# Preparing a block's tokens three blocks ahead, and their remainder behind the second layer's sums

## The chip, the cores and the metric

The kernel runs on one core of a Trainium2 chip. The core has a matrix engine (PE), a vector engine (DVE), an activation engine (ACT), a general engine (POOL), and an engine that issues most DMAs (SP). Each takes its own row of instructions in order; semaphores hold them together. The metric is the device time of one execution in microseconds (us); the median of several is given.

## The reference

Attention with a query averaged over pairs of its rows, then a mixture of eight experts with one expert for each token. `x` is the attention's output as 4608 tokens of 512 values; a token goes through the expert with the highest gate, and the result is scaled by the gate:

```python
q_pool = q.reshape(B, H, S // factor, factor, D).mean(axis=3)
attn = softmax(scale * np.matmul(q_pool, k.transpose(0, 1, 3, 2)))   # in short; written out in the reference
x = (attn @ v).transpose(0, 2, 1, 3).reshape(B * S, H * D)
logits = x @ w_gate + modality_bias[modality_id]
e_idx = np.argmax(logits, axis=1)
for e in range(E):
    mask = e_idx == e
    h = np.maximum(x[mask] @ w1[e], 0.0)          # 512 -> 1024
    out[mask] = gate_w[mask, None] * (h @ w2[e])  # 1024 -> 512
```

## The kernel before

The first 700 us or so are attention. While the last pairs run, the tokens are routed: they are sorted by expert, and two lists of row numbers are made, `giA` for the first eight blocks of 256 tokens and `giB` for the rest. What is left of this routing, and the counting for the later list, is a generator named `side`; `beside()` runs one step of it (a few DVE operations of lines 535 to 547, sometimes a small product of line 580).

The expert stage is `run_blocks` (from line 1828). Blocks 0 to 3 are *plain*: `gemm1` four times, `gemm2` four times, PE in fp16 with every operand split into a high half and a remainder (hi x hi, hi x lo, lo x hi). Blocks 4 to 17 are *seven-product* blocks: 2 x 2 block matrices are multiplied with seven products instead of eight, after sums and differences of the operands have been formed. Block 18 has few tokens and other experts; `general` handles leftovers, of which these inputs have none.

One round of the loop over j (line 1886) is `together(j, j + 1)` and then `tail(j + 1)`. `together` takes the first-layer products 11, s2 and s3 of block j + 1, and the second layer of block j in the order 11, 22, 12, s3, s1, s2, s4 (`second`); `tail` takes the other first-layer products of j + 1: 12, s1, 22 and s4. Each first-layer product is 24 matmuls (line 1605), each second-layer product 12 (line 1705). The order on PE, ACT, DVE and POOL is that in which the code issues; the steps of the generators are placed between the products by the loop. The steps of `together` in the loop are numbered s = 0 to 5; the block's own sums and casts stand between them.

What the other engines do in one round:

- POOL: four subtractions or additions of the hidden values of block j (line 1647, in `tail`), the token differences of a later block (line 1535), sometimes one or two additions of weights (line 1432), two gathers (line 1347, 128 rows each), the sum o of the second layer (line 1739), and two scatters of the finished block's halves (line 1591), with a drain behind the second. A scatter to the output starts when the one before it has landed.
- ACT: the casts to fp16 (line 1613), the copy p of the first product (line 1673), the ReLUs (lines 1623 and 1632), scaled copies of the second layer's products (p, o and x, line 1716), weight halves (line 1425), and for a later block the scaled tokens `xr` (line 1532) and their high half `xs` (line 1539).
- DVE: remainders of the casts (line 1617), sums of the first layer (h22, h12, h21 in line 1622; u2, u3 in lines 1693 and 1694), five sums of the second layer (line 1717), weight remainders (line 1426), and for a later block the token remainder (line 1540).
- SP: weight loads into five buffers, and the two transposes of `xs` into the tile `xpart` (line 1544).

The tokens of a block go through `load_x` (the gathers into `xg`, one buffer of each half) and `turn_s` (from line 1523): step 1 copies the gates and scales the tokens on ACT into `xr`; step 2 forms four differences on POOL; step 3 makes the high half on ACT and the remainder on DVE; step 4 issues the transposes. `xr` and `xs` have one buffer, `xpart` two. In round j the kernel before takes these four steps for block j + 2 at s = 0, 1, 3 and 5 (`T_TURN`) and gathers block j + 3 at s = 3; the gather of block 8, the first that uses the second list, stands behind the tail of the round before, after all of `side`.

Of the kernel before, what the change touches and what calls it, by code (L numbers as in the profile page):

```python
# [105 lines left out]
NSA = 4  # L106
NSB = 5
NA = 2 * NSA
# [4 lines left out]
WR = 5  # L113
JOINED = 2
PREP = ((1,) * 8, ((0, 1, 1, 0, 0, 0),) * 6 + ((0,) * 6, (1,) * 6, (1,) * 6) + ((1, 1, 1, 0, 0, 1),) * 4)
T_TURN = (0, 1, 3, 5)
SIDE = 1
PH = 3
PO = 2
GX = 3  # L120
# [1253 lines left out]
def experts(tc, ctx, rt, ident, pre, x2pool, hip, w1, w2, out, side, first):  # L1374
# [16 lines left out]
    def beside():  # L1391
        for _ in range(SIDE):
            next(side, None)
# [131 lines left out]
    def turn_s(j):  # L1525

        b = B[j]
        gates(j)
        r = xq.tile([P, 8, TB], F32, name="xr")
        for h in (0, 1):  # L1530
            x, sc = scaled_x(j, h)
            nc.scalar.activation(r[:, 2 - 2 * h:4 - 2 * h].rearrange("p k n -> p (k n)"), x, AF.Copy, scale=sc)  # L1532
        yield
        for o, x, y in ((4, 0, 2), (6, 1, 0), (5, 1, 4), (7, 3, 5)):
            nc.gpsimd.tensor_tensor(r[:, o], r[:, x], r[:, y], op=ALU.subtract)  # L1535
        yield
        xs = xq.tile([P, 2, 7 * TB], F16, name="xs")
        flat = r[:, 1:8].rearrange("p k n -> p (k n)")
        nc.scalar.copy(xs[:, 0], flat)
        nc.vector.tensor_tensor(xs[:, 1], flat, xs[:, 0], op=ALU.subtract)  # L1540
        yield
        x = b["xo"] = xq.tile([P, 2, 7, 2, P], F16, name="xpart", bufs=2)
        for w in range(2):
            nc.sync.dma_start_transpose(out=x[:, w].rearrange("p k c n -> p (k c) n"), in_=xs[:, w])
        yield
# [113 lines left out]
        put_hi(j, n, t)  # L1659
        put_lo(j, n, t)  # L1660

    def together(i, j):

        def mine(n):
            if i is not None:
                sums(i, n)

        if j is not None:
            b = B[j]
            pa = b["pa"] = bank()  # L1670
            product1(pa, "11", "11", j, True)
            p1 = temp("p1")
            nc.scalar.copy(p1, pa)
            beside()
            mine("s3")
            pb = b["pb"] = bank()
            product1(pb, "s2", "t2", j, True)
            beside()
            pc = b["pc"] = bank()
            product1(pc, "s3", "t3", j, True)  # L1680
            beside()
            mine("s1")
        else:
            mine("s3")
            mine("s1")
        g = second(i) if i is not None else iter(())
        next(g, None)
        mine("s2")
        next(g, None)
        mine("s4")  # L1690
        if j is not None:
            u2, u3 = b["u2"], b["u3"] = temp("u2"), temp("u3")
            nc.vector.tensor_tensor(u2, pb, p1, op=ALU.add)
            nc.vector.tensor_tensor(u3, pc, u2, op=ALU.add)
        yield
        yield from g
# [127 lines left out]
    def step(g, n=1):  # L1824
        for _ in range(n):
            next(g, None)

    def run_blocks():

        plain = range(NSA)  # L1830
        for j in plain:
            for q in range(4):
                B.setdefault(j, {})["w", q] = first["w", q]
        raws = [load(0, w2, q) for q in range(4)]
        load_x(1)
        turn = {1: turn_x(1)}
        prep = chain(combined(1, w1, sets[0]["w1"], (4, 5, 6, 7, 8, 13, 14)), combined(1, w2, sets[0]["w2"], (15, 16, 17, 18, 19, 20, 0)))
        for j in plain:
            for s in range(8):
                if s < 4:  # L1840
                    if j == 0:
                        for k in plain:
                            B[k]["w", 4 + s] = None
                        w = split(raws[s], 9 + s)
                        for k in plain:
                            B[k]["w", 4 + s] = w
                    gemm1(j, s)
                else:
                    gemm2(j, s % 4)
                if j == 0 and s in (1, 2):  # L1850
                    step(turn[1])
                if j:
                    step(prep, PREP[0][s])
                if j and s == T_ST:
                    scatter(j - 1, 1)
                    nc.gpsimd.drain(fusable=False)
                if s == GX:
                    load_x(j + 2)
                    turn[j + 2] = (turn_x if j + 2 < NSA else turn_s)(j + 2)
                if s in T_AHEAD:  # L1860
                    step(turn[j + 2])
                if j + 1 >= NSA and s < 2:
                    step(turn[j + 1])
            if j + 1 < NSA:
                drain(turn[j + 1])
            scaled(j, 0)
            scaled(j, 1)
            scatter(j, 0)
        drain(prep)
        j = NSA  # L1870
        drain(turn[j])
        last = NST - 1
        change = NSA + NSA + NSB
        for k in range(NSA, NST):
            B.setdefault(k, {}).update(sets[k >= change])
        drain(together(None, j))
        scatter(j - 1, 1)
        drain(turn[j + 1])
        load_x(j + 2)
        for _ in tail(j):  # L1880
            beside()
        nc.gpsimd.drain(fusable=False)
        prep = chain(combined(0, w1, sets[1]["w1"], (1, 2, 3, 9, 10, 11, 12)), combined(0, w2, sets[1]["w2"], (7, 8, 6, 13, 5, 4, 14)), few_weights())
        few_x_ = few_x()
        few1, few2 = few_first(NST), few_second(NST)
        for j in range(NSA, NST):
            if j == last:
                drain(few1)
            if j + 2 <= last and j + 2 not in turn:
                turn[j + 2] = turn_s(j + 2)  # L1890
            for s, _ in enumerate(together(j, j + 1 if j < last else None)):
                beside()
                if j + 2 <= last and s in T_TURN:
                    step(turn[j + 2])
                if s == 3 and j + 3 <= last and j + 3 != NA:
                    load_x(j + 3)
                if j == last - 1:
                    step(few_x_)
                step(prep, PREP[1][j - NSA][s] if j < last else 0)
                if s == 4:  # L1900
                    scatter(j, 1)
            if j < last:
                for s, _ in enumerate(tail(j + 1)):
                    beside()
                    beside()
                    if s == 0:
                        scatter(j, 0)
                        nc.gpsimd.drain(fusable=False)
                if j + 3 == NA:
                    drain(side)  # L1910
                    load_x(j + 3)
        scatter(last, 0)
        nc.gpsimd.drain(fusable=False)
        drain(few2)
# [141 lines left out]
```

## Time and profile before

| what | value |
|---|---|
| median of 3 runs | 1205.84 us (1201.77 to 1206.2) |
| the profiled execution's own time | 1206.51 us |
| its span in the trace | 1204.8 us |
| PE busy over the span | 1076.6 us, 89% |
| DVE, ACT, POOL busy | 969.9, 872.8, 623.1 us (81%, 72%, 52%) |
| mean clock granted to PE | 0.961 of full speed |

The shares are averages over two different stages. Up to about 775 us PE is busy all the time; from there on it is busy 60 to 80% of each stretch, and all the other engines are idle for a part of each block. In such a stage the shares say little: one looks for what ended each wait of PE, and follows that back. A row of the trace reads: start in us, duration in us, engine, line, operation, output<-inputs; in brackets the idle time of the engine just before, and what ended it.

### The profile page before, as it was taken

The numbers are of one execution on the slowest core, as the hardware profiler recorded it, in microseconds if no ns is written. First come the engines' busy times: TensorE is split into PE (matmuls) and PEld (weight loads), VectorE is DVE, ScalarE is ACT, GpSimd is POOL, SyncE is SP. The second block draws the span as 40 slices with busy tenths as digits, with TensorE's granted clock in tenths as the row PEclk, the third lists the DMA queues.
The fourth block names the chain that finished last, engine by engine and source line by source line (L and its number), as shares of the span: only waits on it lengthen the run. The fifth ranks groups of instructions, "written<-read, shape, count | busy, mean of one in ns | idle before, by whom it ended". The sixth has DMA issues, their size and how long they took to land. (4 is left out here: it accounts for less than half of the span.)

```text
span 1204.8 us, 39654 instructions
## 1 busy us (share of the span) xinstructions
PE 1076.6 (89%) x16809; PEld 865.5 (72%) x16809; DVE 969.9 (81%) x1778; ACT 872.8 (72%) x1506; POOL 623.1 (52%) x610
## 2 busy tenths in 40 slices
PE   7999999999999999999999999968867778567875
PEld 3777777777777777677777788867756667567774
DVE  7999999999999999999999974895645656466674
ACT  5899999999999999999999964433434544345542
POOL 7755445454544545445453215664556655665533
PEclk9999999999999999999999999998988999789898
DMA  7787887898888789788876744464243224654321
GB/s 224 184 185 199 191 214 185 193 191 178 201 192 210 178 200 185 174 205 188 195 164 140 200 144 125 129 141 82 70 102 66 67 66 102 102 118 102 84 69 37
DMA packets 181868, 180.19 MB, mean 150 GB/s; under 512 B 113999, under 2 KB 144735, under 8 KB 181680
## 3 DMA queue, kind: packets, MB, share of 16 engines
q1 hardware_dynamic: 171414, 149.22, 52.0%
q0 software_dynamic: 10256, 28.33, 10.8%
q8 instruction: 133, 2.18, 0.8%
q14 instruction: 55, 0.45, 0.1%
q10 hardware_dynamic: 10, 0.00, 0.0%
HBM read 100.30 MB, written 18.98 MB: 99 GB/s over the span
## 5 line engine op out<-in xcount | busy, mean ns | idle before, releaser
L1023 ACT ACTIVATE Pe<-psc 128x432 int32<-128x432 f32 x768 | 376.8, 528 | 37.6 <-PE psc L1022 22.9
L1081 PE MATMUL xp<-VH,Pe 128*128 128x65 f16 x2880 | 345.1, 194 | 0.0
L1082 PE MATMUL xp<-vl,Pe 128*128 128x64 f16 x2880 | 343.6, 192 | 0.0
L1083 PE MATMUL xp<-VS,Pl 128*128 128x65 f16 x2880 | 343.1, 193 | 0.3 <-DVE Pl L1006 0.3
L1081 PEld LDWEIGHTS <-Pe 128*128 128x128 f16 x2880 | 266.5, 97 | 92.8 <-issue 49.6
L946 DVE TENSOR_REDUCE mp<-pm 128x2 f32<-128x1024 f32 (+3 forms) x319 | 296.6, 937 | 20.2 <-PE pm L964 16.4
L1021 PE MATMUL psc<-B 128*128 128x432 f16 (+2 forms) x1152 | 302.2, 286 | 0.9 <-ACT Pe L1023 0.8
L1022 PE MATMUL psc<-B 128*128 128x432 f16 (+2 forms) x1152 | 299.6, 285 | 2.7 <-DMA B<-mr 2.7
L1082 PEld LDWEIGHTS <-Pe 128*128 128x128 f16 x2880 | 265.9, 98 | 42.7
L1083 PEld LDWEIGHTS <-Pl 128*128 128x128 f16 x2880 | 266.2, 97 | 0.5 <-DVE Pl L1006 0.5
L1004 ACT ACTIVATE Pl<-Pe 128x1152 f16<-128x1152 uint16 x186 | 216.5, 1164 | 5.9
L867 POOL TENSOR_SCALAR VH<-rawv,sc 128x512 f16<-128x512 f32 (+1 forms) x60 | 104.0, 1734 | 42.6 <-DVE Pl L1006 39.8
L1022 PEld LDWEIGHTS <-B 128*128 128x128 f16 x1152 | 112.5, 98 | 10.8 <-issue 2.8
L1021 PEld LDWEIGHTS <-B 128*128 128x128 f16 x1152 | 111.1, 97 | 7.8 <-issue 2.4
L728 POOL TENSOR_TENSOR rawq<-rawq 128x576 f32<-128x576 f32 x31 | 43.7, 1408 | 119.2 <-DVE Pl L1006 113.7
L775 POOL TENSOR_TENSOR lo<-rawk,hi 128x576 f16<-128x576 f32 (+1 forms) x68 | 81.6, 1221 | 43.1 <-DVE Pl L1006 34.2
L1006 DVE TENSOR_SCALAR Pl<-Pe 128x576 f16<-128x576 uint16 (+1 forms) x198 | 93.2, 472 | 5.7 <-ACT Pe L1023 5.4
L946 DVE TENSOR_REDUCE mp<-xp 128x1 f32<-128x512 f32 x116 | 78.9, 680 | 0.0
L964 PE MATMUL pm<-hi,qh 64*128 64x512 f16 x348 | 70.0, 383 | 1.1 <-DVE mp L946 1.1
L1535 POOL TENSOR_TENSOR xr<-xr 128x256 f32<-128x256 f32 x56 | 52.1, 951 | 32.9 <-ACT xr L1532 31.8
L1623 ACT ACTIVATE h<-h 128x512 f32<-128x512 f32 x42 | 26.4, 629 | 57.0 <-DVE h L1622 56.8
L1647 POOL TENSOR_TENSOR h<-h,h 128x512 f32<-128x512 f32 x42 | 62.3, 1483 | 3.3
(533 smaller groups left out, 2577.4 us busy)
## 6 DMA issues: line engine op xcount, KB each, us to landing
B<-hi SPq DMA_DIRECT2D x128, 144.0 KB
rawv<-in_att_dram SPq DMA_DIRECT2D x32, 576.0 KB
rawq<-in_att_dram SPq DMA_DIRECT2D x31, 576.0 KB
rawk<-in_att_dram SPq DMA_DIRECT2D x31, 576.0 KB
raw<-in_w_dram SPq DMA_DIRECT2D x28, 512.0 KB
B<-qh SPq DMA_DIRECT2D x128, 72.0 KB
B<-lo SPq DMA_DIRECT2D x64, 144.0 KB
xs<-x SPq DMA_DIRECT2D x15, 576.0 KB
```

The costliest lines, as they stand in the source:

```text
L775: done = (nc.gpsimd if p < 2 or i in LO_POOL else nc.vector).tensor_tensor(o[:, r], t[:, r], h[:, r], op=ALU.subtract)
L867: done = nc.gpsimd.tensor_scalar(vh, v, s["sc"], None, op0=ALU.mult)
L946: most = lambda o, x: nc.vector.tensor_reduce(o, x, op=ALU.max, axis=AX.X)
L964: nc.tensor.matmul(banks[to], queries(j, what), hi[half[j], t * 512:(t + 1) * 512], start=True, stop=True)
L1004: nc.scalar.activation(low, rest, AF.Copy, scale=LOW)
L1006: fast[0] = (nc.vector if eng == 'D' else nc.gpsimd).tensor_single_scalar(low, rest, LOW, op=ALU.mult)
L1021: nc.tensor.matmul(o, b1[:, ks], b1[:, qs], start=True, stop=False, skip_group_check=True)
L1022: nc.tensor.matmul(o, b2[:, ks], b2[:, qs], start=False, stop=True, skip_group_check=True)
L1023: nc.scalar.activation(Pe[:, D + x0:D + x1], pt, AF.Exp, scale=1.0 / 16)
L1081: nc.tensor.matmul(out, Ph[:, qs], vh[:, c, j, 0:D + 1], start=c == 0 and g == 0, stop=False, skip_group_check=True)
L1082: nc.tensor.matmul(out[:, 0:D], Ph[:, qs], vl[:, c, j], start=False, stop=False, skip_group_check=True)
L1083: nc.tensor.matmul(out, Pl[:, qs], vs[:, c, j, 0:D + 1], start=False, stop=c == NKC - 1, skip_group_check=True)
```

## The change

`turn_s` yields once more: ACT's high half is one step, and DVE's remainder together with the transposes the next. In round j these steps are now taken for block j + 3. The first, gates and scaling, is handed to `together` as `scaling` and stands right behind the copy p of product 11, ahead of the casts of the round; the differences come at s = 0, the high half at s = 3, the remainder and the transposes at s = 5, behind the second layer's sums. Block j + 4 is gathered at s = 3. For block 8 what is left of `side` is run in front of that gather, in round 4. So that the first rounds find their tokens ready, blocks 4 and 5 are prepared in the plain blocks and block 6 in the round that fills the pipeline, and each step of the plain blocks runs one more step of `side`. In the last rounds there is less to prepare: round 14 gathers nothing, rounds 15 and 16 prepare nothing of this kind.

Because one line was added near the top and two further down, the lines after the change read one to two higher: 1539 is 1540, 1540 is 1542, 1622 is 1623, 1717 is 1719.

```diff
@@ -113,7 +113,8 @@
 WR = 5
 JOINED = 2
 PREP = ((1,) * 8, ((0, 1, 1, 0, 0, 0),) * 6 + ((0,) * 6, (1,) * 6, (1,) * 6) + ((1, 1, 1, 0, 0, 1),) * 4)
-T_TURN = (0, 1, 3, 5)
+T_TURN = (0, 3, 5)
+T_GX = 3
 SIDE = 1
 PH = 3
 PO = 2
@@ -1537,8 +1538,8 @@
         xs = xq.tile([P, 2, 7 * TB], F16, name="xs")
         flat = r[:, 1:8].rearrange("p k n -> p (k n)")
         nc.scalar.copy(xs[:, 0], flat)
+        yield
         nc.vector.tensor_tensor(xs[:, 1], flat, xs[:, 0], op=ALU.subtract)
-        yield
         x = b["xo"] = xq.tile([P, 2, 7, 2, P], F16, name="xpart", bufs=2)
         for w in range(2):
             nc.sync.dma_start_transpose(out=x[:, w].rearrange("p k c n -> p (k c) n"), in_=xs[:, w])
@@ -1659,7 +1660,7 @@
         put_hi(j, n, t)
         put_lo(j, n, t)
 
-    def together(i, j):
+    def together(i, j, scaling=iter(())):
 
         def mine(n):
             if i is not None:
@@ -1672,6 +1673,7 @@
             p1 = temp("p1")
             nc.scalar.copy(p1, pa)
             beside()
+            step(scaling)
             mine("s3")
             pb = b["pb"] = bank()
             product1(pb, "s2", "t2", j, True)
@@ -1836,17 +1838,17 @@
         turn = {1: turn_x(1)}
         prep = chain(combined(1, w1, sets[0]["w1"], (4, 5, 6, 7, 8, 13, 14)), combined(1, w2, sets[0]["w2"], (15, 16, 17, 18, 19, 20, 0)))
         for j in plain:
+            k = j + 2
             for s in range(8):
                 if s < 4:
                     if j == 0:
-                        for k in plain:
-                            B[k]["w", 4 + s] = None
                         w = split(raws[s], 9 + s)
-                        for k in plain:
-                            B[k]["w", 4 + s] = w
+                        for m in plain:
+                            B[m]["w", 4 + s] = w
                     gemm1(j, s)
                 else:
                     gemm2(j, s % 4)
+                beside()
                 if j == 0 and s in (1, 2):
                     step(turn[1])
                 if j:
@@ -1854,13 +1856,21 @@
                 if j and s == T_ST:
                     scatter(j - 1, 1)
                     nc.gpsimd.drain(fusable=False)
-                if s == GX:
-                    load_x(j + 2)
-                    turn[j + 2] = (turn_x if j + 2 < NSA else turn_s)(j + 2)
-                if s in T_AHEAD:
-                    step(turn[j + 2])
-                if j + 1 >= NSA and s < 2:
-                    step(turn[j + 1])
+                if k <= NSA and s == GX:
+                    load_x(k)
+                    turn[k] = (turn_x if k < NSA else turn_s)(k)
+                if s in T_AHEAD and k <= NSA:
+                    step(turn[k])
+                if j == NSA - 1:
+                    if s < 3:
+                        step(turn[NSA])
+                    if s == 0:
+                        load_x(NSA + 1)
+                        turn[NSA + 1] = turn_s(NSA + 1)
+                    if s > 3:
+                        step(turn[NSA + 1])
+                    if s == 6:
+                        load_x(NSA + 2)
             if j + 1 < NSA:
                 drain(turn[j + 1])
             scaled(j, 0)
@@ -1869,16 +1879,23 @@
         drain(prep)
         j = NSA
         drain(turn[j])
+        drain(turn[j + 1])
         last = NST - 1
         change = NSA + NSA + NSB
         for k in range(NSA, NST):
             B.setdefault(k, {}).update(sets[k >= change])
+            if k > NSA + 1:
+                turn[k] = turn_s(k)
         drain(together(None, j))
+        step(turn[j + 2])
+        load_x(j + 3)
+        step(turn[j + 2])
         scatter(j - 1, 1)
-        drain(turn[j + 1])
-        load_x(j + 2)
-        for _ in tail(j):
+        for s, _ in enumerate(tail(j)):
             beside()
+            if s == 1:
+                step(turn[j + 2])
+        drain(turn[j + 2])
         nc.gpsimd.drain(fusable=False)
         prep = chain(combined(0, w1, sets[1]["w1"], (1, 2, 3, 9, 10, 11, 12)), combined(0, w2, sets[1]["w2"], (7, 8, 6, 13, 5, 4, 14)), few_weights())
         few_x_ = few_x()
@@ -1886,14 +1903,15 @@
         for j in range(NSA, NST):
             if j == last:
                 drain(few1)
-            if j + 2 <= last and j + 2 not in turn:
-                turn[j + 2] = turn_s(j + 2)
-            for s, _ in enumerate(together(j, j + 1 if j < last else None)):
+            x = turn.get(j + 3, iter(()))
+            for s, _ in enumerate(together(j, j + 1 if j < last else None, x)):
                 beside()
-                if j + 2 <= last and s in T_TURN:
-                    step(turn[j + 2])
-                if s == 3 and j + 3 <= last and j + 3 != NA:
-                    load_x(j + 3)
+                if s in T_TURN:
+                    step(x)
+                if s == T_GX and j + 4 <= last:
+                    if j + 4 == NA:
+                        drain(side)
+                    load_x(j + 4)
                 if j == last - 1:
                     step(few_x_)
                 step(prep, PREP[1][j - NSA][s] if j < last else 0)
@@ -1906,9 +1924,6 @@
                     if s == 0:
                         scatter(j, 0)
                         nc.gpsimd.drain(fusable=False)
-                if j + 3 == NA:
-                    drain(side)
-                    load_x(j + 3)
         scatter(last, 0)
         nc.gpsimd.drain(fusable=False)
         drain(few2)
```

On DVE, the round of block 13 before (it runs from 1080.70 us on; w15 and w16 are weight halves, xs the token remainder, u and o the second layer's five sums, the last row h22):

```order
L1694 TENSOR_TENSOR u_22468<-ph,u_22467 128x512
L1498 COPY gate<-xg_22162 128x1
L1498 COPY gate<-xg_22164 128x1
L1426 SCALAR_TENSOR_TENSOR w15l<-raw,w15h 128x1024
L1540 TENSOR_TENSOR xs<-xr,xs 128x1792
L1717 SCALAR_TENSOR_TENSOR u_22557<-po_22428,gate,p_22444 128x256
L1717 SCALAR_TENSOR_TENSOR u_22558<-po_22429,gate,u_22557 128x256
L1717 SCALAR_TENSOR_TENSOR o_22427<-po_22429,gate,u_22558 128x256
L1717 SCALAR_TENSOR_TENSOR u_22556<-po_22428,gate,p_22443 128x256
L1717 SCALAR_TENSOR_TENSOR o_22426<-po_22430,gate,u_22556 128x256
L1426 SCALAR_TENSOR_TENSOR w16l<-raw,w16h 128x1024
L1622 TENSOR_TENSOR h_22641<-ph,u_22468 128x512
```

and after the change:

```order
L1696 TENSOR_TENSOR u_22494<-ph,u_22493 128x512
L1427 SCALAR_TENSOR_TENSOR w15l<-raw,w15h 128x1024
L1719 SCALAR_TENSOR_TENSOR u_22576<-po_22454,gate,p_22470 128x256
L1719 SCALAR_TENSOR_TENSOR u_22577<-po_22455,gate,u_22576 128x256
L1719 SCALAR_TENSOR_TENSOR o_22453<-po_22455,gate,u_22577 128x256
L1719 SCALAR_TENSOR_TENSOR u_22575<-po_22454,gate,p_22469 128x256
L1719 SCALAR_TENSOR_TENSOR o_22452<-po_22456,gate,u_22575 128x256
L1542 TENSOR_TENSOR xs<-xr,xs 128x1792
L1427 SCALAR_TENSOR_TENSOR w16l<-raw,w16h 128x1024
L1623 TENSOR_TENSOR h_22661<-ph,u_22494 128x512
```

The remainder (xs) has moved from the front of the five sums to behind them, still ahead of the weight half and of h22, and the two gate copies have left this place.

On ACT, the front of the same round before (p is the copy of product 11, hs3h to hs4h the casts of the hidden sums, xr the scaled tokens):

```order
L1673 COPY p_22366<-ph 128x512
L1613 CAST hs3h<-hs_22331 128x512
L1613 CAST hs1h<-h_22328 128x512
L1716 ACTIVATE p_22443<-po_22428,gate 128x256
L1716 ACTIVATE p_22444<-po_22428,gate 128x256
L1613 CAST hs2h<-h_22237 128x512
L1613 CAST hs4h<-h_22297 128x512
L1532 ACTIVATE xr<-xg_22162 128x512
L1532 ACTIVATE xr<-xg_22164 128x512
```

and after the change:

```order
L1674 COPY p_22386<-ph 128x512
L1533 ACTIVATE xr<-xg_22181 128x512
L1533 ACTIVATE xr<-xg_22183 128x512
L1614 CAST hs3h<-hs_22351 128x512
L1614 CAST hs1h<-h_22348 128x512
L1718 ACTIVATE p_22469<-po_22454,gate 128x256
L1718 ACTIVATE p_22470<-po_22454,gate 128x256
L1614 CAST hs2h<-h_22257 128x512
L1614 CAST hs4h<-h_22317 128x512
```

The two scalings stand now right behind p, ahead of all four casts, and they are those of a block one further ahead.

## Rows read from the trace of the kernel before

**Rows 1.** Two stretches: busy us of PE, PEld, DVE, ACT, POOL; clock, DMA, GB/s.

```profile
750.00:775.00 25.00, 25.00 (x231) 22.41 (x230) 20.89 (x52) 10.42 (x14) 15.36 (x11) 1.00 0.45 138
...
1025.00:1050.00 25.00, 12.26 (x152) 11.96 (x150) 10.92 (x14) 8.30 (x12) 13.14 (x11) 0.66 0.74 122
```

**Rows 2.** Waits of PE from 770 us: line waited for, total us, times, longest.

```profile
PE ph L1605 <- DVE h L1622: 47.0, 10, 9.2
PE ph L1605 <- DMA xpart<-xs: 21.9, 10, 4.1
PE po L1705 <- ACT x L1716: 13.0, 5, 4.9
PE po L1705 <- ACT p L1716: 10.5, 8, 1.9
```

**Rows 3.** PE: starts of two first-layer products.

```profile
794.56 1.50 PE L1605 MATMUL ph<-xpart,xfirst 128*128 128x128 f16 x24
795.90 0.28 PE L1605 MATMUL ph<-xpart,x 128*128 128x128 f16 x2
```

**Rows 4.** PE: starts of two second-layer products in the round of block 13.

```profile
1084.74 0.38 PE L1705 MATMUL po<-x,h12h 128*128 128x256 f16 x2 [1.44 <-ACT p L1716]
...
1086.04 0.38 PE L1705 MATMUL po<-x,hs3h 128*128 128x256 f16 x2
```

**Rows 5.** POOL in other rounds: first subtractions, differences, addition, gather, scatters.

```profile
809.43 1.26 POOL L1647 TENSOR_TENSOR hs<-h,h 128x512 f32<-128x512 f32 x1 [0.33 <-ACT h L1623]
...
823.60 2.90 POOL L1535 TENSOR_TENSOR xr<-xr 128x256 f32<-128x256 f32 x4 [8.37 <-ACT xr L1532]
826.46 2.35 POOL L1432 TENSOR_TENSOR raw<-raw 128x1024 f32<-128x1024 f32 x1
828.95 2.58 POOL L1347 DMA_INDIRECT xg<-xs,giA  x1
...
852.33 4.75 POOL L1535 TENSOR_TENSOR xr<-xr 128x256 f32<-128x256 f32 x4 [1.97 <-ACT xr L1532]
...
1035.57 1.01 POOL L1591 DMA_INDIRECT out_dram<-o,siB  x1 [0.16 <-POOL raw L1432]
1045.55 0.99 POOL L1591 DMA_INDIRECT out_dram<-o,siB  x1 [8.97 <-DMA out_dram<-o,siB]
...
1150.50 0.99 POOL L1591 DMA_INDIRECT out_dram<-o,siB  x1 [0.43 <-DVE u L1717]
1154.13 1.02 POOL L1591 DMA_INDIRECT out_dram<-o,siB  x1 [2.64 <-DMA out_dram<-o,siB]
...
1179.63 1.26 POOL L1647 TENSOR_TENSOR hs<-h,h 128x512 f32<-128x512 f32 x1 [2.00 <-ACT few L1764]
```

**Rows 6.** POOL in the round of block 13, in order of time.

```profile
1080.70 1.26 POOL L1647 TENSOR_TENSOR hs<-h,h 128x512 f32<-128x512 f32 x1 [2.05 <-issue]
1082.03 4.61 POOL L1647 TENSOR_TENSOR h<-h,h 128x512 f32<-128x512 f32 x3
1088.61 3.88 POOL L1535 TENSOR_TENSOR xr<-xr 128x256 f32<-128x256 f32 x4 [1.97 <-ACT xr L1532]
1092.64 0.98 POOL L1347 DMA_INDIRECT xg<-xs,giB  x1
...
1097.33 0.72 POOL L1739 TENSOR_TENSOR o<-x,u 128x256 f32<-128x256 f32 x1 [2.43 <-DVE u L1717]
1098.51 1.00 POOL L1591 DMA_INDIRECT out_dram<-o,siB  x1 [0.46 <-DVE u L1717]
1103.98 0.99 POOL L1591 DMA_INDIRECT out_dram<-o,siB  x1 [4.47 <-DVE h L1622]
1107.03 1.26 POOL L1647 TENSOR_TENSOR hs<-h,h 128x512 f32<-128x512 f32 x1 [2.05 <-issue]
```

**Rows 7.** ACT's copy of the high half in that round.

```profile
1092.52 1.69 ACT L1539 CAST xs<-xr 128x1792 f16<-128x1792 f32 x1 [2.32 <-POOL xr L1535]
```

**Rows 8.** DVE's remainder in that round.

```profile
1094.24 2.02 DVE L1540 TENSOR_TENSOR xs<-xr,xs 128x1792 f16<-128x1792 f32 x1 [3.13 <-ACT xs L1539]
```

## The prediction

> **What bounds the kernel now.** I read the waits of PE from 770 us on first, then the busy time by stretch, then one block instruction by instruction on POOL, ACT, DVE and PE. Before 775 us PE is busy in every microsecond [rows 1], so nothing that other engines do there can shorten the time; the change can win only behind it, in the fourteen seven-product blocks. There PE waits, and the waits have names [rows 2]: ten for a sum h22 on DVE (47.0 us), ten for the transposed tokens of the next block (21.9 us), then ACT's scaled copies x and p (13.0 and 10.5 us). PE has fourteen products in a block: a first-layer product takes 795.90 - 794.56 = 1.34 us, a second-layer one 1086.04 - 1084.74 = 1.30 us [rows 3, 4], together 7 x 1.34 + 7 x 1.30 = 18.5 us. A block takes more: POOL's first subtraction of line 1647 starts at 809.43 us in the first of these blocks and at 1179.63 us in the last [rows 5, 6], thirteen periods in 370.2 us, 28.5 us on average.
>
> The waits on PE are ends of a ring that runs through POOL. In the block that starts at 1080.70 us [rows 6] POOL does its four subtractions (to 1086.64), idles 1.97 us for ACT's scaled tokens, makes four differences of tokens (3.88 us), issues two gathers, idles 2.43 us for DVE's sum u, adds (0.72 us), issues the first scatter at 1098.51, and can issue the second only at 1103.98, when the first has landed. 0.99 us of issue and 2.05 us of drain later the next block begins, at 1107.03. ACT's copy xs waits 2.32 us for those differences [rows 7]; DVE's remainder, 2.02 us after an idle of 3.13 us [rows 8], stands in front of the second layer's five sums, which is why POOL waits for u, and the same five sums stand in front of h22, for which PE waits.
>
> **The change, part by part.** *Scaling ahead of hs3h.* ACT's two scaled copies (the first ends the 1.97 us of idle on POOL) move ahead of four casts. They then lie in the time in which ACT waits for POOL's first subtraction anyway; POOL finds the tokens ready and the 1.97 us goes. *Remainder behind the sums.* DVE does the five sums first, so POOL's 2.43 us for u goes as well: u needs PE's second-layer product s2, the fifth of the stage, whose group ends about 9.3 us after POOL's first subtraction (12 starts 1084.74 - 1080.70 = 4.04 us after it, then four products of 1.30 us), plus two sums, some 10.5 us; POOL itself comes free at 11.95 us (5.94 + 3.4 + 2.6, below). Where there is nothing to gather, u decides. *Transposes a block ahead.* They are issued when PE has left the old tile, a whole block before use; the 21.9 us cannot stay as such. SP's weight loads behind them move by the length of two transposes, and their buffers are used only in the block after. *Gathers.* The same two per block, at the same step, one block further ahead; the one at the change from the first to the second index list, which stood at the end of a block, is now issued in the step of the others. *Side work.* A third call per step in the plain blocks pulls the rest of the routing into a stretch where DVE is busy 20.89 of 25 us and PE 25.00 [rows 1]. Cost: nothing if DVE's 4 us of room in that stretch and the larger room before it take it; at worst the same DVE work stalls PE for a few products, up to 4 us; below zero too, since PE has this work taken off the later blocks. I take 0.
>
> So what is left of a block is POOL's own row of work. Its fixed part: 5.94 (four subtractions) + 0.72 (add) + 0.46 (idle in front of the scatter) + 0.99 + 2.05 = 10.16 us [rows 6]. The four differences cost 2.90 us alone and 4.75 us beside DVE's long operations [rows 5]; they now follow straight on the subtractions, beside two of DVE's casts, so I take 3.4. That these two engines get in each other's way is a rule of the Trainium skill too (GPSIMD Engine Reference, Specifications: the SBUF interfaces are shared with VectorE, with contention where DVE reads two SBUF inputs), and it speaks against the new place, since the casts' remainders read two. By that rule alone each of eleven blocks would pay 4.75, and the time would be 15 us longer than I forecast; the row of 2.90 us shows that the differences also find free time.
>
> Two gathers run from 1092.64 to 1097.33 - 2.43 = 1094.90, 2.6 us with the gaps around them [rows 6]; one of them alone took 2.58 us beside the remainder on DVE, and a weight addition takes 2.35 us [rows 5]. The largest unknown is L, from the first scatter's issue to the second's: 5.47 us in the block shown [rows 6], 3.63 us where no gather ran, 9.98 us in the block with the most weight loads [rows 5]. Today the transposes of the same block run beside that landing; they leave it, but the gathers come nearer. I keep it at about what each kind has today.
> - Four blocks with a gather and no weight addition: 10.16 + 3.4 + 2.6 + L 5.5 = 21.7 us each, 86.7 us.
> - Four with one addition (2.35) and gathers between those two cases (3.3): L 6.2, 25.4 us each, 101.6 us.
> - Two with two additions: 10.16 + 3.4 + 4.7 + 3.5 + L 8.8 = 30.5 us each, 61 us.
> - Two late ones without a gather: u decides, 10.5 + 0.72 + 0.46 + 3.65 + 3.04 = 18.4 us, hardly over PE's 18.5: 19 us each, 38 us.
> - The one before last has no token work today either: 22.5 us stays (from 1154.13 + 1.02 and the 2 us of drain to 1179.63 [rows 5]).
>
> Together 309.8 us against 370.2: 60.4 us less. PE then waits 3 to 7 us in most blocks, in one place (ACT's p, before the product 12). After long waits the granted clock is lower, 0.66 of the full 2.4 GHz on average in the worst stretch [rows 1], which is much of it at the lower level of 1.2 GHz, where a product takes longer; POOL's row covers most of that, and I give back 4 us. Nothing is booked for the attention stage or for the end. The profiled execution took 1206.51 us, of which 1204.8 us is span; its distance to the median 1205.84 us is 0.7 us and I leave it. 1206.5 - 60.4 + 4 = **1150 us**.
>
> **Rivals.** *A: the landing follows the gathers.* In the block shown the second scatter starts 9.1 us after the last gather's issue ends; without a gather it starts 3.63 us after the first scatter. If the scatter's data queue behind the gathers' data, what counts is the gather's end, and the idle for u was free. Then a block is 5.94 + 3.4 + 2.6 + 9 + 3.04 = 24.0 us, with an addition 27.0 us, the two heavy ones 31: 15 us more than forecast, 1165 us. For it: L is long just where gathers stand close. Against it: the transposes that shared that time leave.
> *B: h22 stays late.* The remainder is still ahead of h22 on DVE. Differences at 4.75 us put its end at 5.94 + 4.75 + 1.69 + 2.02 = 14.4 us, against 13.2 us when PE has the first product for h22; with ACT's copy behind x as well, PE would keep about half of the 47.0 us. Only the transposes' 21.9 us and a little more go: 1180 us.
> *C: PE bounds.* If L drops to 3.7 us with the transposes gone, the ten lighter blocks come near PE's 18.5 us: 10 x 18.8 + 61 + 22.5 = 271.5 us, 1108 us.
> *D: slower.* One copy buffer holds the tokens: ACT's copy for the next block must wait until both transposes of the last have landed, and these now stand in SP's row behind PE's tail. ACT takes its work in order, so the split of weights and the ReLU behind that copy wait with it, then h22, the tail and POOL. Differences end 9.3 us into a block, so a landing before that costs nothing. If it comes only 20 us into the block, behind a weight load that waits for its buffer, a block takes some 20 + 1.7 + 2.0 + 8 = 32 us (8 us: from the remainder's end at 1096.26 to 1107.03, less the five sums [rows 6, 8]), in eleven blocks 11 x (32 - 28.5) = 38 us more than now: 1245 us. It turns slower than now from about 17 us. Against it: the old tile is free before the block begins.
> *E: no change.* If POOL's waits just move into L in every block, the period stays: 1201 to 1206 us.
>
> **How the numbers follow.** Forecast 0.47, A 0.20, B 0.11, C 0.10, E 0.07, D 0.05. The likeliest is 1150 us. The range reaches from halfway to C over A to B with its bounds: 1118 to 1185 us; outside are the lower half of C, D and E. Half a percent, 6 us, is about what a measurement of this kernel can tell from no change; faster by more than that has 0.88, within it 0.07, slower 0.05.
>
> **What would show it.** PE's wait for xpart gone from the list; its wait for h22 under 15 us; its wait for ACT's p grown to some 40 us; POOL's idle in front of the differences gone and that for u under 10 us; block periods of 21 to 25 us, with the two heavy blocks near 30. A is right if the second scatter still starts about 9 us after the gathers; B if h22 leads the list; D if ACT idles in front of its copy for a DMA. The forecast is wrong above all if L is not what it was.

## The result, and the profile after

The changed kernel takes 1173.5 us (median of 4 runs, 1170.12 to 1175.51) against 1204.41 us before: a ratio of 0.9742, with a 95% interval of 0.9711 to 0.9774, or 31 us less. The forecast was 1150 us; so the direction and the range held, and the time is 23.5 us above it. The profiled execution took 1172.89 us with a span of 1171.2 us.

PE's waits in the changed kernel from 770 us on, to be held against [rows 2] (line waited for, total, times, longest; a line of before reads one or two higher here):

```profile
PE po L1707 <- ACT p L1718: 33.1, 10, 6.9
PE ph L1606 <- DVE h L1623: 16.1, 7, 8.4
PE po L1707 <- ACT x L1718: 12.8, 4, 5.1
PE ph L1606 <- ACT p L1674: 3.5, 1, 3.5
PE ph L1606 <- DMA xpart<-xs: 2.4, 1, 2.4
```

The wait for the transposes is nearly gone (21.9 us to 2.4 us, one wait), h22 has fallen from 47.0 to 16.1 us, and ACT's p has taken the first place: it comes late because the casts in front of it wait for POOL's first subtraction. So PE's waits have moved to where POOL's row sets the round. POOL in the round of block 13, the same round as [rows 6]:

```profile
1053.54 1.29 POOL L1648 TENSOR_TENSOR hs<-h,h 128x512 f32<-128x512 f32 x1 [2.46 <-ACT h12h L1614]
1054.91 4.62 POOL L1648 TENSOR_TENSOR h<-h,h 128x512 f32<-128x512 f32 x3
1059.50 4.83 POOL L1536 TENSOR_TENSOR xr<-xr 128x256 f32<-128x256 f32 x4
1064.48 0.99 POOL L1348 DMA_INDIRECT xg<-xs,giB  x1 [0.15 <-issue]
1065.77 0.96 POOL L1348 DMA_INDIRECT xg<-xs,giB  x1 [0.30 <-DVE u L1719]
1066.75 0.73 POOL L1741 TENSOR_TENSOR o<-x,u 128x256 f32<-128x256 f32 x1
1067.77 2.50 POOL L1592 DMA_INDIRECT out_dram<-o,siB  x1 [0.28 <-POOL o L1741]
1073.29 1.01 POOL L1592 DMA_INDIRECT out_dram<-o,siB  x1 [3.02 <-DVE h11l L1618]
1078.35 1.26 POOL L1648 TENSOR_TENSOR hs<-h,h 128x512 f32<-128x512 f32 x1 [4.06 <-issue]
```

The two idle times that the change was to remove are removed: nothing lies ahead of the differences (before 1.97 us), nothing ahead of the sum o (before 2.43 us). The first scatter is issued 14.23 us into the round, before 17.81 us. But the round is 24.81 us long, before 26.33 us: of 4.4 us of idle time removed, 1.5 us are left. The rest is lost in two places in these rows. The differences take 4.83 us (before 3.88), and behind the second scatter POOL stands for 4.06 us where it stood for 2.05. The issue of the first scatter is longer as well, 2.50 us (before 1.00), but the second scatter follows the first by 5.52 us, before by 5.47, so that the longer issue is no loss against before in this round; it stands where a gain was to be had, as a later run shows.

The fourteen first subtractions now start at 815.78 to 1142.97 us, thirteen periods in 327.2 us (before 370.2, forecast 309.8). The first of them comes 6.35 us later than before, and from the last to the end of the span it takes 28.2 us, before 25.2.

### The profile page after: what moved, and what is told of

Read it like the earlier page. It is cut to its first block, busy times and chain, and to the rows that moved or that the text cites. A ratio compares the mean times of both kernels' runs of the same rounds, so it can differ in the third digit from the quotient of the medians.

```text
span 1171.2 us, 39664 instructions
## 1 busy us (share of the span) xinstructions
PE 1071.8 (92%) x16809; PEld 857.0 (73%) x16809; DVE 967.6 (83%) x1778; ACT 872.9 (75%) x1506; POOL 639.9 (55%) x610
## 5 line engine op out<-in xcount | busy, mean ns | idle before, releaser
L1536 POOL TENSOR_TENSOR xr<-xr 128x256 f32<-128x256 f32 x56 | 58.1, 1056 | 6.6 <-DVE w20l L1427 2.6
L1618 DVE TENSOR_TENSOR hs3l<-hs,hs3h 128x512 f16<-128x512 f32 x14 | 16.0, 1144 | 50.8 <-ACT hs3h L1614 50.8
```

## The experiments

Each run was measured together with the kernel before, and its ratio is to that kernel, with the 95% interval in brackets. "By the ratios" means: the difference of two ratios times 1204.41 us; it is uncertain by some 5 us.

The theory (T) for the largest of the losses: the drain that POOL does behind the second scatter waits until that scatter has landed, and the transposes, which the change moved to this very moment, lengthen that landing. The rival (S): POOL is held up by DVE on a shared way to memory, and the transposes are bystanders. What spoke for T is the round of block 4 of the changed kernel, on POOL and then on SP:

```profile
834.54 1.02 POOL L1592 DMA_INDIRECT out_dram<-o,siA  x1 [0.28 <-POOL o L1741]
838.16 1.39 POOL L1592 DMA_INDIRECT out_dram<-o,siA  x1 [2.60 <-DVE h22l L1618]
844.02 1.26 POOL L1648 TENSOR_TENSOR hs<-h,h 128x512 f32<-128x512 f32 x1 [4.46 <-issue]
```

```profile
835.98 3.79 SPq L1545 DMA_TRANSPOSE xpart<-xs  x2
```

The second scatter is issued at 838.16 us, while SP is issuing the two transposes (835.98 to 839.77 us); the next subtraction starts 5.86 us later. Of that one scatter the trace gives the time from issue to landing (smallest, median, largest; one instruction):

```profile
DMA to landing us min/median/max: 5.6/5.6/5.6
```

and of its counterpart in the kernel before:

```profile
DMA to landing us min/median/max: 2.7/2.7/2.7
```

In the kernel before the next subtraction started 3.0 to 3.5 us after the second scatter in thirteen rounds, always 0.2 to 0.4 us after it had landed (2.7 to 3.2 us); after the change it starts 3.05 to 5.89 us after it, and in the six rounds whose landing is recorded again 0.2 to 0.4 us behind it. That reads as a landing, and not as a fixed drain of 2 us; the runs that follow try it.

**Transposes held back.** The transposes are a step of their own, issued behind the tail, and wait for POOL's first subtraction of the next round; a block still has a whole round for them.

```diff
             nc.vector.tensor_tensor(xs[:, 1], flat, xs[:, 0], op=ALU.subtract)
+            yield
...
...
+            t = nc.sync.dma_start_transpose(out=x[:, w].rearrange("p k c n -> p (k c) n"), in_=xs[:, w])
+            if "behind" in b:
+                tc.add_manual_dep(t.ins, b["behind"].ins.name, mybir.DependencyInfo(mybir.DependencyClass.Sync, mybir.DependencyReason.DATA))
...
-        sub(b["hs3"], h21, h11)
+        b["first"] = sub(b["hs3"], h21, h11)
...
+                if j + 3 <= last:
+                    B[j + 3]["behind"] = B[j + 1]["first"]
+                step(x)
```

> The changed kernel, with the two transposes of a block held back on SP until POOL's first subtraction of the next round has run, that is until the second scatter and the drain behind it are over; nothing else is moved. Theory T: the drain behind the second scatter waits until that scatter has landed, and the transposes, which now start at the same moment, lengthen that landing from 2.7 to up to 5.6 us; then the time from the second scatter's issue to the next subtraction goes back to about 3.05 us in every round and the kernel takes about 12 us less, 1161 us. Rival S: POOL is held up by VectorE on the shared way to memory, the transposes are bystanders: 1173 us, and the 4 to 6 us behind the second scatter stay.

Measured: 1157.39 us, ratio 0.9624 (0.9581 to 0.9668): 14 us less than the change by the ratios. The round of block 4, on POOL and SP:

```profile
835.00 1.01 POOL L1595 DMA_INDIRECT out_dram<-o,siA  x1 [0.48 <-DVE u L1722]
839.41 1.05 POOL L1595 DMA_INDIRECT out_dram<-o,siA  x1 [3.40 <-DVE h L1626]
842.51 1.27 POOL L1651 TENSOR_TENSOR hs<-h,h 128x512 f32<-128x512 f32 x1 [2.06 <-ACT xr L1533]
```

```profile
843.81 3.68 SPq L1546 DMA_TRANSPOSE xpart<-xs  x2
```

The transposes now start behind the subtraction, and the subtraction follows the second scatter by 3.10 us, as before the change. Over the thirteen rounds the time behind the second scatter falls from 54.9 to 43.4 us. In two rounds it stays above the 3.05 us that were expected (4.01 us in block 6 and 4.78 us in block 14). T holds, S does not.

**No transposes.**

```diff
+        if j > NSA + 2:
+            b["xo"] = B[NSA + 2]["xo"]
+            yield
+            return
         x = b["xo"] = xq.tile([P, 2, 7, 2, P], F16, name="xpart", bufs=2)
```

> The changed kernel without the transposes of blocks 7 to 17: these blocks read the turned tokens of block 6 (part of the work is left out). Theory T: no transposes, so the second landing is 2.7 to 3.2 us in every round and the kernel takes 12 to 15 us less than 1173, about 1160 us. Rival S: the time behind the second scatter stays as it is, 1172 us.

Measured: 1158.48 us, ratio 0.963 (0.959 to 0.967), the same as with the transposes held back, and the time behind the second scatter is 43.4 us again. So the price of the transposes lies in that landing; what they cost elsewhere is too small for these runs to tell. One round does not fit: in block 14 of this kernel, which has no transposes, the second scatter (1085.47 us) landed only after 4.5 us and the next subtraction followed it by 4.69 us. What lengthened that landing is open.

**No drain.**

```diff
                     if s == 0:
                         scatter(j, 0)
-                        nc.gpsimd.drain(fusable=False)
```

> The changed kernel without the drain that POOL does behind the second scatter of a round. Theory T: the drain is a wait for the landing; without it POOL goes on some 1.2 us after the scatter's issue, 2 to 4.5 us earlier in each of 12 rounds, as far as PE's sums are there: 20 to 35 us less than 1173, about 1147 us, and PE's wait for ACT's p falls from 33 us to under 15. Rival S: the next subtraction waits for the writing of descriptors in any case; within 4 us of 1173.

Measured: 1148.8 us, ratio 0.954 (0.9504 to 0.9576), 24 us less than the change by the ratios. POOL in the round of block 4, and PE's two waits that belong to it:

```profile
840.02 1.05 POOL L1592 DMA_INDIRECT out_dram<-o,siA  x1 [3.39 <-DVE h L1623]
841.55 1.27 POOL L1648 TENSOR_TENSOR hs<-h,h 128x512 f32<-128x512 f32 x1 [0.47 <-ACT h L1624]
```

```profile
PE ph L1606 <- DVE h L1623: 17.9, 7, 8.4
...
PE po L1707 <- ACT p L1718: 9.9, 6, 5.6
```

The subtraction follows the scatter by 1.53 us, and what ends its idle time is ACT's ReLU, that is PE's own product. PE's wait for ACT's p falls from 33.1 to 9.9 us. In five of the thirteen rounds the subtraction now follows the scatter by 1.0 to 1.1 us, which is the scatter's issue alone. The drain itself, not the writing of the scatter's descriptors, was the wait.

**Both.**

> Both edits at once: transposes held back until POOL's first subtraction, and no drain. Theory T: without the drain the second landing is waited for by nothing until the next round's first scatter, so holding the transposes back has nothing left to win: the same as without the drain alone, within 4 us, about 1147 us. Rival S: within 4 us of 1173.

Measured: 1146.17 us, ratio 0.9526 (0.9489 to 0.9563), inside the interval of the run without the drain alone, as T has it. It has the lowest ratio of all, 58 us under the kernel before in its own measurement, but the intervals do not tell it from the other changed kernels without the drain.

**The remainder put back** (ahead of the second layer's sums; the rest of the change stays).

```diff
         nc.scalar.copy(xs[:, 0], flat)
-        yield
         nc.vector.tensor_tensor(xs[:, 1], flat, xs[:, 0], op=ALU.subtract)
+        yield
```

> The changed kernel with one part undone: DVE's remainder stands again directly behind ACT's copy, ahead of the second layer's sums; the transposes stay where the change put them. If the remainder's place is what the change wins by, POOL's wait for u and PE's wait for h22 come back, up to 2 us in each of eleven rounds: 1185 to 1195 us. Rival: POOL is bound by the landings, and DVE comes in time either way: 1170 to 1177 us; the first scatter's issue, which now takes 2.5 us where it runs beside the remainder, would then be short again.

Measured: 1191.4 us, ratio 0.9922 (0.9896 to 0.9948), 22 us more than the change by the ratios. In the trace 6.4 us of that lie ahead of the first subtraction (822.22 us against 815.78). POOL in the round of block 13:

```profile
1080.82 0.96 POOL L1348 DMA_INDIRECT xg<-xs,giB  x1 [0.31 <-issue]
1084.22 0.73 POOL L1741 TENSOR_TENSOR o<-x,u 128x256 f32<-128x256 f32 x1 [2.44 <-DVE u L1719]
1085.40 1.02 POOL L1592 DMA_INDIRECT out_dram<-o,siB  x1 [0.46 <-DVE u L1719]
1089.02 1.04 POOL L1592 DMA_INDIRECT out_dram<-o,siB  x1 [2.61 <-DMA out_dram<-o,siB]
```

The 2.44 us for u are back, and PE's wait for h22 is back at 38.1 us. Two things in these rows were not in the sum. The scatter's issue takes 1.02 us again, and 1.00 to 1.02 us in all thirteen rounds: the 2.50 us of the changed kernel are the price of the remainder's new place, for there DVE's remainder (1066.88 us, 2.50 us long) runs beside that issue, which starts at 1067.77 us. And the second scatter follows the first by 3.62 us although the issue of two gathers ended only 3.6 us ahead of the first; in twelve of the thirteen rounds of this kernel, with gathers or without, it is 3.54 to 4.17 us. The gathers do not show in that landing.

**The scaling put back** (behind the four casts).

```diff
-            for s, _ in enumerate(together(j, j + 1 if j < last else None, x)):
+            for s, _ in enumerate(together(j, j + 1 if j < last else None)):
                 beside()
+                if s == 0:
+                    step(x)
```

> The changed kernel with another part undone: ACT scales the tokens at the first step of the round again, behind the four casts, and no longer ahead of hs3h. If this part wins what the sum booked for it, POOL idles 1.97 us in front of the differences in eleven rounds: 1190 to 1196 us. Rival: the time comes back in the landing behind it: 1172 to 1178 us.

Measured: 1187.34 us, ratio 0.9902 (0.9865 to 0.9939), 19 us more than the change by the ratios. Undone one at a time, the two parts cost 41 us together, more than the 31 that the whole change brought, so they do not add up. The page has the 56 quarter differences in one row, first of the changed kernel, then of this one (busy us, mean ns of one, idle before):

```profile
L1536 POOL TENSOR_TENSOR xr<-xr 128x256 f32<-128x256 f32 x56 | 58.1, 1056 | 6.6 <-DVE w20l L1427 2.6
```

```profile
L1536 POOL TENSOR_TENSOR xr<-xr 128x256 f32<-128x256 f32 x56 | 49.1, 897 | 27.7 <-ACT xr L1533 21.6
```

The scaling's early place removes 21.6 us of idle on POOL and makes the differences 9.0 us dearer. These two net to some 12 of the 19.4 us by which the thirteen rounds of this trace are longer (346.6 us against 327.2); the rest is not assigned. In the changed kernel seven of the eleven groups of differences took 4.83 us, four 3.79 or 4.10 us, none the 2.9 us of the shortest. What stands beside them on DVE tells the two sizes apart: always remainders of the casts, and in the seven groups of 4.83 us, block 13's among them, a weight remainder too. Block 10 has none. First block 10's differences, then block 13's weight remainder:

```profile
976.99 3.79 POOL L1536 TENSOR_TENSOR xr<-xr 128x256 f32<-128x256 f32 x4
...
1062.53 1.22 DVE L1427 SCALAR_TENSOR_TENSOR w15l<-raw,w15h 128x1024 f16<-128x1024 f32 x1
```

No run took DVE's work away from there, so this cause is read from the rows. All these remainders read two SBUF inputs. The Trainium skill (GPSIMD Engine Reference, Specifications), as named in the prediction, states that POOL shares its SBUF interfaces with VectorE, with contention where DVE reads two SBUF inputs. The trace agrees with it: 3.79 to 4.83 us beside such remainders, where the prediction took 3.4.

**The side work put back.**

```diff
                     gemm2(j, s % 4)
-                beside()
```

> The changed kernel without the third call of the side work in the plain blocks, so that more of the routing runs behind them, and the rest in front of the gather of block 8. The sum booked nothing for it: 1172 to 1176 us. If the denser side work costs the plain blocks time, it is 2 to 4 us faster; if the routing behind them is what it avoids, 3 to 8 us slower.

Measured: 1173.16 us, ratio 0.9788 (0.9753 to 0.9822). The interval overlaps that of the change, so the times alone settle nothing. The traces say where a difference would come from. The plain blocks take as long with the third call as without: from the attention's last product to the first seven-product one 88.5 us in the changed kernel, 88.0 us here. But the round of block 4 takes 32.55 us here against 28.24, because POOL's first gather of that round waits for the rest of the routing:

```profile
834.03 0.97 POOL L1348 DMA_INDIRECT xg<-xs,giB  x1 [3.28 <-DVE mB L598]
```

So the third call seems to bring some 4 us, read from one execution of each kernel.

**The kernel before, without the drain** (the same line taken out).

> The kernel before without the drain behind the second scatter of a round. Theory T (the drain waits for the landing, 2.7 us at least): POOL gains about 2 us in each of thirteen rounds and is the ring's bound there too: 1180 us, about 25 us less than before. Rival: before the change PE's waits for h22 and for the transposes set the round, and they are not POOL's: 1200 us.

Measured: 1179.22 us, ratio 0.985 (0.9791 to 0.9909), 18 us less (11 to 25 by the interval). One line less in the old kernel wins some 60% of what the whole change won. POOL in the round of block 13 and the start of the next:

```profile
1078.36 0.99 POOL L1591 DMA_INDIRECT out_dram<-o,siB  x1 [5.44 <-DVE h12l L1617]
1079.37 1.28 POOL L1647 TENSOR_TENSOR hs<-h,h 128x512 f32<-128x512 f32 x1
```

There is no idle time between the two, where [rows 6] has 2.05 us. So the drain was a price of the kernel before too, and not only of what the change did.

**The second scatter behind the subtractions, no drain.**

```diff
-                    if s == 0:
+                    if s == 3:
                         scatter(j, 0)
-                        nc.gpsimd.drain(fusable=False)
```

> The changed kernel without the drain and with the second scatter moved behind the four subtractions of line 1648, so that POOL does not wait for the first landing ahead of them. If POOL's ring of landings is what still sets the rounds once the drain is gone, POOL's row of work falls to some 17 us in a round (5.9 + 4.8 + 2.6 + 0.7 + 0.5 + 2 x 1.0, or 2.4 more with a weight addition), under PE's 18.5, and the kernel takes 10 to 20 us less than without the drain alone: 1130 to 1140 us. Rival: without the drain PE's own sums (h21 and the ReLU behind it) already release POOL, and nothing is left to win there: 1145 to 1150 us.

Measured: 1146.36 us, ratio 0.9545 (0.9507 to 0.9583), not to be told from the kernel without the drain alone. The 10 to 20 us did not come; the rival was right. POOL's waits say why:

```profile
POOL hs L1648 <- ACT h L1624: 63.1, 14, 6.1
```

In all fourteen rounds POOL now waits for the ReLU of h21, the end of PE's tail. Without the drain and with the scatter out of the way, what releases POOL is PE's product and ACT's ReLU behind it, and the scatters lie beside that path.

**The same with the transposes held back.**

> The same, with the transposes also held back until POOL's first subtraction. The first landing no longer stands in POOL's way, so where the transposes run should not matter: the same as with the second scatter moved alone, within 4 us. If they still lengthen something that PE waits for, such as the gathers' landing, it differs by more.

Measured: 1149.49 us, ratio 0.9576 (0.9537 to 0.9615), 3 us from the second scatter moved alone, within the 4 us that were expected.

## Why the prediction was right in its direction and its range, and short by 23 us

**What bounds the kernel.** Right: the ring through POOL. The chain of reasoning from PE's waits to POOL's two idle times held, and both parts of the change that address them are worth about 20 us each, by the two runs that undo them one at a time.

**The transposes a block ahead.** Half right. PE hardly waits for them any more (2.4 us). But I followed only who waits for the transposes, and of their traffic I said that it leaves the first scatter's landing. I did not ask what it meets in its new place.

**The fixed part of POOL's row.** This is the step that failed. The sum has "0.99 + 2.05" for the second scatter and its drain in every round, 39.5 us in thirteen. It measured 54.9 us: the drain is no fixed time but waits for the landing, and the transposes came to lie on it. The row in [rows 6] gave "issue" as what ended the idle time, which says only that the profile shows no waited-for event; that it was much the same in every round (1.97 to 2.14 us) looked like a constant, but each time it was the end of a landing, 2.7 to 3.2 us counted from the issue. Holding the transposes back returned 14 us, leaving out the drain 24 us.

**The differences.** 3.4 us was too low: eleven of them took 49.3 us, against 37.4 at 3.4 us each. In the ten rounds for which the sum books them that is 10.4 us more; in block 14 the sum goes by u. The choice leaned on the row of 2.90 us, in a place that has two remainders of casts beside it and in seven of the eleven rounds a weight remainder too; the row of 4.75 us was the nearer one.

**L, from the first scatter to the second.** 75.4 us in the sum, 60.8 us measured, 14.5 us less. The sum kept it at what each kind of round had before, when the transposes ran beside that landing; they left it, and with the remainder put back L is 48.8 us in all. That the transposes lengthened it before is likely, but no run puts them alone back beside it. The 12 us between 48.8 and 60.8 fit in the main the issue of 2.5 to 2.6 us beside the remainder: in the six rounds that have it L is 5.06 to 5.52 us. Rival A, whose blocks add up to 17 us over the forecast and not 15, is refuted: in the round shown the second scatter follows the last gather by 6.6 us (1065.77 + 0.96 to 1073.29), not 9.1, and with the remainder put back L is 3.6 us with gathers or without.

Together: 309.8 + 15.4 (behind the second scatter) + 10.4 (differences) - 14.5 (L) = 321.1 us; 327.2 measured. Of the other 6.1 us, 3.1 are a wait for u in block 12, where the sum had none, and 2.3 lie in block 14, where u comes late and the first scatter is issued 14.6 us into the round; the rest is small. That the time fell well inside the range owes something to luck: L, which the prediction called its largest unknown, was off by as much as the second scatter's landing, the other way. The whole miss is then 17.4 us in the thirteen rounds and 9.4 us ahead of them and behind them, less the 4 us booked for the clock.

**Booked at nothing, and not nothing.** The first seven-product round starts 6.35 us later and the end after the last one takes 3.1 us longer. 2.1 us of the first were there when the plain blocks ended (the first seven-product product starts at 795.31 us, before at 793.22), and the attention's last product had already started 2.4 us later (706.8 against 704.4 us), where the change moves nothing. So the plain blocks took no longer, and where the attention ends varies from one execution to the next (704.9 us with the side work put back, whose first subtraction is as late, at 815.83 us). The rest lies between: block 6's differences (3.40 us) now stand on POOL ahead of the first round; that they are the cause is read from the order, not tried. For the end no run tells the cause.

**The 4 us for the clock** do not appear as a term of their own. The granted clock over the span went from 0.961 to 0.970. That POOL's row covered the slow products is not shown by any run.

**The other rivals.** B (h22 stays late): its mechanism shows only in the two rounds with most weight work, 8.4 and 4.4 us of the 16.1. C (PE bounds) is approached when the drain goes too, at 1146 us and not at 1108: with both edits PE's product releases POOL in eight of the thirteen rounds, but C's ten lighter rounds take 18.3 to 24.6 us, 218.6 us together against the 188 of its sum; the two heavy ones, 58.5 us, do not exceed it. D did not occur: ACT never waited for its copy buffer; once, for 4.0 us, its scaling waited for the tile that DVE's remainder still read. **The signs:** the transposes' wait and the idle ahead of the differences came out as said, the p wait reached 33.1 us of some 40; the rounds of blocks 4, 6 and 7 took 27.2 to 28.2 us, above the 21 to 25; h22 missed its 15 us by one; the idle for u is 25.9 us and not under 10: 22.1 us of it lie in the last four rounds, which had it before too and were left out of that sign.

## What to carry to other kernels

When a transfer is moved out of one wait's way, look up what is in flight at its new place and who waits for that to land; the engine that issues it tells nothing of it. A time that is the same in every round need not be a cost of its own: ask whether it is the floor of something that can grow. And before a ring of engines that wait for each other is re-ordered, take out one by one the waits in it that no data ask for: one line, a drain, was worth 24 us on top of a re-ordering that brought 31.

## What the runs showed of the hardware that was not expected

- A drain on POOL behind an indirect scatter held POOL until the scatter had landed: the next operation started 0.2 to 0.4 us behind the landing in all nineteen rounds with a recorded landing, from 2.7 to 5.6 us. Without the drain, and where nothing else held it, it started 1.0 us after the scatter's issue began.
- The second scatter of a round, 128 rows of 2 KB, landed in 2.7 to 3.2 us in the kernel before, with no transposes beside it, and in 3.2 to 5.6 us in the five recorded rounds after the change in which two transposes of SBUF tiles were issued around it. With no transposes there was one landing of 4.5 us, in block 14, which stays unexplained. Gathers in front of a scatter did not show: with the remainder put back the two scatters were 3.6 us apart with and without them.
- The issue of an indirect scatter on POOL took 1.0 us alone and 2.5 us beside a DVE subtraction that reads two SBUF operands, and the DVE operation was longer by 0.5 us (2.50 against 2.02 us).
- Four POOL subtractions of 128x256 took 2.9 us at the shortest, 3.79 us beside two DVE remainders of casts, and 4.83 us when a DVE weight remainder ran beside them as well.
